# Eight plain products for the first group of batch 1, and the spatial weights' combinations made over a longer stretch

## The chip, the cores and the metric

One NeuronCore of a Trainium2 chip runs the whole program. The metric is the time of one execution on the device, in microseconds. The engines are named as the profile names them: PE is TensorE's matmuls, PEld its weight loads, DVE is VectorE, ACT is ScalarE, POOL is GpSimd, SP the engine that issues all DMAs of this kernel. Each works through its own instructions in order.

## The reference

Three layers follow one another, on 4 batches of 1088 tokens: a linear attention with polynomial features (4 heads of 32), a gated mixture layer (128 to 1024 to 128, shifted tokens), and a gMLP, the part that the change is in:

```python
h = np.maximum(x @ w_in, 0.0)                 # (4, 1088, 1024)
u, v = (h[..., :512], h[..., 512:])
mu = np.mean(v, axis=-1, keepdims=True)
var = np.mean((v - mu) ** 2, axis=-1, keepdims=True)
v_n = (v - mu) / np.sqrt(var + 1e-06)
v_s = np.einsum('ts,bsd->btd', w_spatial, v_n) + b_spatial[None, :, None]
gated = u * v_s
return (gated @ w_out).astype(np.float32)
```

The large product is `w_spatial` (1088 x 1088) with `v_n`, for each batch.

## The kernel before

**Number format.** A float32 operand is split into a high and a low part (`copy` on ScalarE makes the high part, `low` subtracts it from the whole), and `mm3` makes each product from three matmuls: low by high, high by high, high by low. `mm3` holds line 123, on which most matmul rows stand; line 126 is `copy`, line 129 is `low`.

**The spatial product.** The result is computed transposed, 128 channels `d` (four blocks) by tokens in three column chunks `c` of 384, 384 and 320 columns. The source tokens are eight blocks `k` of 128, and a tail of 64 that goes with the bias through tiles T1 and T2 (`tmm`, lines 683 and 684, and lines 537 and 538).

**Batch 0** does it plainly in twelve units `u` (`spatial`, order `ORD0`): a unit makes the window matmuls of u (left operands winH and winL, bank 3), the 24 weight matmuls of one `d` and one `c`, the tail's two, then `L539` on VectorE multiplies the accumulator by the gate, and `put_out` splits the product into high and low (`gH` on ScalarE, `gL` on VectorE). The output projection's three matmuls (left operands woL and woH; the third one needs `gL`) are kept in the list `gout` and are issued in the next unit, after its k = 6. Units 4 and 5 are (d 2, c 0) and (d 3, c 0), 6 and 7 are c 1 of the same, 8 to 11 are c 2 of all four blocks. Between the matmuls of a unit, a list `fill` places other work: the v tiles of batch 1 (`v_tile`: 512-column matmuls, ReLU, statistics on VectorE, a power on GpSimd, then `v_rest`, line 471, and a store to DRAM) two in each of the units 5 to 8, and the weight combinations of the table `W2`.

**Batches 1 to 3** work in groups (b, p), each for two channel blocks, d = p and e = p + 2. `group` is a generator, and each of its `yield`s ends a step, after which the loop at the program's end places other work. The first two column chunks and the two halves of the source tokens form a 2 by 2 block product, which a Strassen-Winograd scheme makes with seven block products for eight (`prod`; a block product is four k by three matmuls of 384 columns). The third chunk is done plainly (`plain`). A group needs

- the v blocks 11, 12, 22, 21 and their combinations 2, 1, 3, 4, made by `build(b, p, i)` in the order of `BUILD` from quadrants that `quad_load` fetches back from DRAM into slots of the buffer `VR`. Each build is a copy on ScalarE and a subtraction on GpSimd; 2 takes three sums on VectorE more, 4 takes one. The results rotate through four buffers `n1H`, `n1L`, `k0`, `k1`;
- the weights' blocks 11, 12, 21, 22 as batch 0 left them, and the combinations 1 = W12 - W11, 3 = W22 - W12, 2 = W11 + 3 and 4 = W21 - 2 for each of the four k (`ctile`). They are made once, from raw float32 weights that are loaded a second time: for each k, `first_load` and `first_sums` make 1, `second_load` and `second_sums` make 3, 2 and 4. Combination 4 takes the place of block 12 (`wtile(k, 1)`), so it can't be made before the last plain use of column chunk 1. `tail_sums` makes the difference of the tail's first two chunks from `btail`.

Each sum is one subtraction or addition on VectorE (line 587, `tt`), followed by `parts`: a copy on ScalarE and a subtraction on GpSimd. Raw weights stand in slots of `VR`.

**Order.** The program text gives the order in which work is wanted; a planner with a timeline of its own then sets each engine's order, so that instructions near one another in the text can change places on an engine. `xsplit(2)` (four copies and four splits on VectorE, line 129) stands ahead of group (1,0). In groups with p = 0 each step also makes one v tile of the next batch.

Of the kernel before, what the change touches and what calls it, by code (L numbers as in the profile page):

```python
# [8 lines left out]
F32 = mybir.dt.float32  # L9
# [49 lines left out]
W1G = 69  # L59
W1N = 8  # L60
ORD0 = ((0, 0), (1, 0), (0, 1), (1, 1), (2, 0), (3, 0), (2, 1), (3, 1), (0, 2), (1, 2), (2, 2), (3, 2))
W2 = {4: ((1, "fl", 0), (3, "fl", 1)), 5: ((3, "fs", 0), (4, "fl", 2), (6, "fs", 1), (7, "fl", 3)),
      6: ((3, "fs", 2),), 7: ((1, "fs", 3), (2, "sl", 2)), 8: ((3, "ss", 2), (4, "sl", 0)),
      9: ((1, "ss", 0), (6, "sl", 1)), 10: ((2, "ss", 1), (7, "sl", 3)), 11: ((3, "ss", 3),)}
SSET = {2: (3, 4, 5, 6), 0: (7, 8, 5, 6), 1: (7, 8, 5, 6), 3: (7, 8, 5, 6)}
R0 = (1, 5)
R1 = 5
VW = NH * (HD + 1)
# [1 line left out]
RING = ("n1H", "n1L", "k0", "k1")  # L70
BUILD = (11, 12, 22, 21, 2, 1, 3, 4)
CHOME = {(1, 2): ("t0",), (3, 2): ("t1",), (1, 3): ("t2",), (3, 3): ("t3",), (1, 0): ("t4",), (3, 0): ("x0",),
         (1, 1): ("x1",), (3, 1): ("xrH", "xrL"), (2, 0): ("n0H",), (2, 1): ("n0L",), (2, 2): ("m14", "mx"),
         (2, 3): ("st0", "st1"), (5, NK): ("m12", "m13")}


@with_exitstack
def attn_moe_gmlp(ctx: ExitStack, tc: tile.TileContext, qT, kT, va, st, wk, wv, wr, win, wout,
# [10 lines left out]
    def sb(tag, shape, dt=F32):  # L89
        uid[0] += 1  # L90
        return pool.tile(shape, dt, tag=tag, bufs=1, name=f"{tag}_{uid[0]}")

    def bank(i):
        uid[0] += 1
        return pp.tile([128, 512], F32, tag=f"p{i}", bufs=1, name=f"p{i}_{uid[0]}")
# [3 lines left out]
    def rot(*tags):  # L99
        i = count.get(tags, 0)  # L100
        count[tags] = i + 1
        return tags[i % len(tags)]

    def m(i):
        return f"m{i}"
# [14 lines left out]
    def mm3(out_ap, lH, lL, rH, rL, first, last, late=1, skip=False):  # L120
        parts = [(lL, rH), (lH, rH), (lH, rL)]
        for n, (l, r) in enumerate(parts if late else parts[::-1]):
            TE.matmul(out_ap, lhsT=l, rhs=r, start=first and n == 0, stop=last and n == 2, skip_group_check=skip)  # L123
# [290 lines left out]
    def wtile(k, c):  # L414
        n = CH[c][1]
        for t, _ in wplace(k, c):
            if t not in wt:
                wt[t] = sb(f"w{t}", [128, S], F32R)
        return [wt[t][:, o:o + n] for t, o in wplace(k, c)]
# [161 lines left out]
    def wraw(dst, n, k):  # L581
        o = CH[n % 10 - 1][0]
        r = 128 * (k + HALF * (n // 10 - 1))
        nc.sync.dma_start(out=dst, in_=wT[r:r + 128, o:o + CMAX])

    def tt(eng, o, a, b_, op):
        return eng.tensor_tensor(out=o, in0=a, in1=b_, op=op)  # L587
# [3 lines left out]
    def stage(j):  # L591
        return VR[:, j, :CMAX]

    def first_load(k):
        raws[1, k] = [stage(j) for j in rot((3, 4), (5, 6), (7, 8))]
        for x, n in zip(raws[1, k], (11, 12)):
            wraw(x, n, k)

    def parts(n, k, src):
        H, L = ctile(n, k)  # L600
        copy(H, src)
        low(GE, L, src, H)

    def first_sums(k):
        r11, r12 = raws.pop((1, k))
        tt(VE, r11, r12, r11, ALU.subtract)
        parts(1, k, r11)

    def second_load(k):
        raws[2, k] = [stage(j) for j in SSET[k]]  # L610
        for x, n in zip(raws[2, k], (12, 22, 11, 21)):
            wraw(x, n, k)

    def second_sums(k):
        r12, r22, r11, r21 = raws.pop((2, k))
        tt(VE, r22, r22, r12, ALU.subtract)
        parts(3, k, r22)
        tt(VE, r11, r22, r11, ALU.add)
        parts(2, k, r11)
        tt(VE, r21, r21, r11, ALU.subtract)  # L620
        parts(4, k, r21)

    def tail_sums():
        H, L = ctile(5, NK)
        x, y = sb(m(10), [128, CMAX]), sb(m(11), [128, CMAX])
        nc.sync.dma_start(out=x, in_=btail[:, :CMAX])
        nc.sync.dma_start(out=y, in_=btail[:, CMAX:2 * CMAX])
        tt(VE, x, x, y, ALU.subtract)
        parts(5, NK, x)
        VE.tensor_copy(L[64:65], H[64:65].bitcast(F32))  # L630
        copy(H[64:128], H[0:64].bitcast(F32))
# [24 lines left out]
    def group(b, p):  # L656
# [16 lines left out]
            for k in range(HALF):  # L673
                mm3(acc, v[:, 0, k], v[:, 1, k], *ctile(w, k), first and k == 0, k == HALF - 1, 0, True)

        def plain(acc, a, first):
            v = vset[b, p, a]
            for k in range(HALF):
                mm3(acc, v[:, 0, k], v[:, 1, k], *wtile(k + HALF * (a % 10 - 1), NCH - 1), first and k == 0, False, 0, True)

        def tmm(acc, d, W):
            T1, T2 = tl[b, d]
# [19 lines left out]
                gout.pop(0)()  # L702

        d, e = p, p + 2
        X = bank(0)[:, :CMAX]
        prod(X, 11, 11, True)
        m1 = snap(X)
# [260 lines left out]
    for u, (d, c) in enumerate(ORD0):  # L968
        if u < EARLY:
            continue  # L970
        fill = {}

        def add(k, fn, *a):
            fill.setdefault(k, []).append(lambda: fn(*a))

        for k in range(WB[u] if u < len(WB) else 0):
            add(k, wstep)
        if u == EARLY:
            add(0, xsplit, 1)
        for n, j in enumerate({5: (0, 1), 6: (2, 3), 7: (4, 5), 8: (6, 7)}.get(u, ())):  # L980
            add(2 + 3 * n, v_rest)
            add(2 + 3 * n, v_tile, 1, j)
        for k, fn, *a in W2.get(u, ()):
            add(k, {"fl": first_load, "fs": first_sums, "sl": second_load, "ss": second_sums}[fn], *a)
        if u == 9:
            add(2, v_rest)
            for n in (11, 12):
                add(2, quad_load, 1, 0, n)
        if u == 10:
            add(2, tails, 1, 0, vtail[:, 0])  # L990
            add(4, build, 1, 0, 0)
        if u == 11:
            add(1, build, 1, 0, 1)
            for n in (22, 21):
                add(7, quad_load, 1, 0, n)
        spatial(0, d, c, fill)
    assert wi[0] >= len(worder) and not pending_raw
    groups = [(b, p) for b in range(1, B) for p in range(2)]
    for gi, (b, p) in enumerate(groups):
        nxt = groups[gi + 1] if gi + 1 < len(groups) else None  # L1000
        if gi == 0:
            build(1, 0, 2)
            tails(1, 2, vtail[:, 0])
            build(1, 0, 3)
            tail_sums()
        if p == 0 and b + 1 < B:
            xsplit(b + 1)
        for st, _ in enumerate(group(b, p)):
            if st < 4:
                build(b, p, st + 4)  # L1010
            elif nxt:
                build(*nxt, st - 4)
            if nxt:
                if st in (1, 2):
                    quad_load(*nxt, (11, 12)[st - 1])
                if st in (3, 4):
                    quad_load(*nxt, (22, 21)[st - 3])
                if st in (3, 4):
                    tails(nxt[0], nxt[1] + 2 * (st - 3), vtail[:, 0])
            v_rest()  # L1020
            if b + 1 < B:
                if p == 0:
                    v_tile(b + 1, st, (3, 7))
                elif st == 0 and b % 2:
                    v_tile(b + 1, NK, (3, 7))
    while gout:
        gout.pop(0)()
# [56 lines left out]
```

## Time and profile before

| | us |
|---|---|
| median of three runs | 466.0 |
| lowest and highest | 465.8, 466.21 |
| the profiled execution, in all | 466.96 |
| its span in the profile | 465.2 |

The profile shows one execution. Busy time is the time in which an engine has an instruction under way; a matmul's end is modelled, so matmul rows overlap and their durations are no price: the price of a matmul is read from the distance of two starts. The granted clock is the share of TensorE's full speed that it was given.

### The profile page before, as it was taken

To read this page: it belongs to the slowest core of one execution; us is meant where nothing else is said; L and a number is where in the kernel's file an instruction comes from. 1 tells how busy PE (TensorE), PEld (TensorE's weight loads), DVE (VectorE), ACT (ScalarE), POOL (GpSimd) and SP (SyncE) were. 2 spreads that over 40 slices of the span, in tenths; PEclk is the share of its full clock that TensorE was granted. 3 is DMA by queue.
4 is the path that set the end of the run, shared out by engine and by line. 5 is a ranking of instruction groups with operands and counts; after the bars stand their busy time and mean duration, and the time that the engine had idled before them with its cause. 6 is when DMAs were issued, how large, how long until landed. Compare 5 with 4: busy or idle time off the path is not lost.

```text
span 465.2 us, 7573 instructions
## 1 busy us (share of the span) xinstructions
PE 446.7 (96%) x2685; PEld 421.0 (90%) x2685; DVE 288.1 (62%) x497; ACT 264.9 (57%) x606; POOL 243.5 (52%) x287
## 2 busy tenths in 40 slices
PE   8978999999999998999999989999999999999997
PEld 7967998989998886999888889999999999999996
DVE  4599768768445796348676567884475971623523
ACT  2585769888766987675444644444464433534322
POOL 2566546586634889539554655634534633425230
PEclk9999999999999999999999989999999999999999
DMA  7973100001100111036534632312112213010001
GB/s 219 345 261 93 49 0 2 17 23 50 41 2 1 36 51 36 11 91 179 153 135 144 180 93 68 115 47 92 59 58 82 100 48 113 14 58 24 0 1 48
DMA packets 32101, 36.49 MB, mean 78 GB/s; under 512 B 2944, under 2 KB 27584, under 8 KB 32064
## 3 DMA queue, kind: packets, MB, share of 16 engines
q1 hardware_dynamic: 32064, 36.01, 24.5%
q8 instruction: 21, 0.34, 0.3%
q14 instruction: 16, 0.13, 0.1%
HBM read 27.48 MB, written 8.52 MB: 77 GB/s over the span
## 4 chain that ended last, share of the span: by engine, by line
PE 64%; DVE 11%; POOL 9%; DMA 8%; issue 3%; ACT 3%; SPq 1%; POOLq 0%; DVEq 0%; ACTq 0%
PE p L123 49%; DMA VR<-in_wT_dram 4%; PE p L397 3%; PE p L231 3%; DVE w L129 3%; PE p L269 3%; PE p L200 2%; POOL m L354 2%; DVE VR L587 1%; DVE VR L471 1%; PE p L684 1%; PE p L683 1%; PE p L252 1%; POOL w L129 1%; DMA w<-in_qT_dram 1%
## 5 line engine op out<-in xcount | busy, mean ns | idle before, releaser
L123 PE MATMUL p<-m,k 128*128 128x384 f32 (+1 forms) x288 | 65.6, 347 | 2.7 <-POOL k L144 1.6
L123 PE MATMUL p<-w,k 128*128 128x384 f32 (+1 forms) x360 | 64.6, 323 | 0.0
L354 POOL TENSOR_TENSOR m<-m 128x384 f32<-128x384 f32 (+1 forms) x48 | 42.8, 897 | 38.0 <-ACT m L351 32.4
L123 PEld LDWEIGHTS p<-w,k 128*128 128x128 f32 x360 | 59.5, 188 | 0.6
L587 DVE TENSOR_TENSOR m<-p,m 128x384 f32<-128x384 f32 (+2 forms) x37 | 18.6, 519 | 58.7 <-PE p L684 57.9
L123 PEld LDWEIGHTS p<-m,k 128*128 128x128 f32 x288 | 48.2, 189 | 6.3 <-POOL k L144 1.8
L129 POOL TENSOR_TENSOR k<-VR,k 128x512 fp32r<-128x512 f32 x26 | 35.1, 1351 | 31.7 <-ACT k L126 28.9
L129 DVE TENSOR_TENSOR w<-m,w 128x384 fp32r<-128x384 f32 (+1 forms) x44 | 32.7, 751 | 28.5 <-POOL m L354 18.4
L351 ACT ACTIVATE m<-p 128x384 f32<-128x384 f32 (+1 forms) x96 | 42.5, 471 | 11.0 <-PE p L123 8.3
L126 ACT ACTIVATE m<-m 128x384 fp32r<-128x384 f32 (+2 forms) x45 | 22.6, 503 | 39.7 <-DVE m L697 24.0
L129 DVE TENSOR_TENSOR m<-m,m 128x384 fp32r<-128x384 f32 (+1 forms) x47 | 33.5, 713 | 16.3 <-ACT m L126 11.0
L471 DVE TENSOR_SCALAR VR<-VR,mv,rs 128x512 f32<-128x512 f32 x33 | 34.1, 1039 | 12.5 <-POOL rs L468 12.2
L123 PE MATMUL p<-w,n1H 128*128 128x384 f32 (+1 forms) x192 | 41.2, 333 | 0.2 <-DVE x L539 0.2
L126 ACT ACTIVATE m<-p 128x384 f32<-128x384 f32 (+2 forms) x39 | 18.3, 471 | 32.7 <-PE p L123 23.4
L587 DVE TENSOR_TENSOR VR<-VR 128x512 f32<-128x512 f32 (+1 forms) x40 | 28.6, 714 | 13.2 <-DMA VR<-in_wT_dram 9.4
L123 PE MATMUL p<-w,n1L 128*128 128x384 f32 (+1 forms) x168 | 34.3, 325 | 0.0
L123 PEld LDWEIGHTS p<-w,n1H 128*128 128x128 f32 x192 | 33.6, 195 | 0.8 <-DVE x L539 0.5
L397 PE MATMUL p<-w,wvT 128*128 128x384 f32 (+1 forms) x88 | 34.3, 471 | 0.0
L126 ACT ACTIVATE k<-VR 128x512 fp32r<-128x512 f32 x26 | 16.3, 630 | 25.0 <-PE p L123 20.2
L123 PEld LDWEIGHTS p<-w,n1L 128*128 128x128 f32 x168 | 28.4, 188 | 0.3
L129 POOL TENSOR_TENSOR n1H<-VR,n1H 128x512 fp32r<-128x512 f32 x12 | 15.5, 1290 | 25.1 <-ACT n1H L126 25.1
L123 PE MATMUL p<-w,xs1H 128*128 128x384 f32 (+1 forms) x88 | 25.1, 339 | 2.9 <-DVE w L129 2.9
(259 smaller groups left out, 1157.3 us busy)
## 6 DMA issues: line engine op xcount, KB each, us to landing
vd<-VR SPq DMA_DIRECT2D x24, 256.0 KB, 2.0
VR<-vd SPq DMA_DIRECT2D x24, 256.0 KB, 3.0
VR<-in_wT_dram SPq DMA_DIRECT2D x24, 192.0 KB, 2.6
st<-in_wT_dram SPq DMA_DIRECT2D x16, 192.0 KB, 2.3
w<-in_kT_dram SPq DMA_DIRECT2D x8, 192.0 KB, 5.1
w<-in_qT_dram SPq DMA_DIRECT2D x8, 192.0 KB, 5.2
out_dram<-m SPq DMA_DIRECT2D x8, 192.0 KB, 1.9
st<-in_wT_dram SPq DMA_DIRECT2D x8, 160.0 KB, 2.3
```

The lines of the kernel that those rows point to most:

```text
L123: TE.matmul(out_ap, lhsT=l, rhs=r, start=first and n == 0, stop=last and n == 2, skip_group_check=skip)
L126: return SE.activation(out=dst, in_=src, func=AF.Copy)
L129: return eng.tensor_tensor(out=L, in0=src, in1=H.bitcast(F32), op=ALU.subtract)
L200: TE.matmul(wide[:, 64 * t:64 * t + 128], lhsT=src[:, cut(c, t, CH[c][0])], rhs=Sbd, start=True, stop=True)
L231: TE.matmul(kv[:, w * g:w * g + w], lhsT=kp, rhs=vt if wide else vt[:, VP * g:VP * g + VP], start=(t == 0), stop=(t == NT - 1))
L252: TE.transpose(pt[:, cut(c, t)], qp[:, t, 128 * g:128 * g + 128], idn)
L269: nd_pe[0] = TE.matmul(o.rearrange("p h c -> p (h c)"), lhsT=qt[g][:, cut(c, t)], rhs=kb[:, g], start=not wide or g == 0, stop=not wide or ...
L351: SE.activation(out=r, in_=hk, func=AF.Relu)
L354: anchor[2] = GE.tensor_tensor(out=sq, in0=r, in1=r, op=ALU.mult)
L397: TE.matmul(vvs[i], lhsT=wvT[:, f // 2], rhs=hls.pop(g), start=f == 0, stop=f == NF - 1)
L471: VE.tensor_scalar(out=v, in0=v, scalar1=mv[:, 0:1], scalar2=rs, op0=ALU.subtract, op1=ALU.mult)
L587: return eng.tensor_tensor(out=o, in0=a, in1=b_, op=op)
```

## The change

In group (1,0), `group` returns early through a new branch: for each of the two channel blocks, and for each of the two v blocks of that block, the three column chunks are done with `plain`, which now takes the chunk as an argument; with the second v block come the window, the tail, the gate and `put_out`. That makes twelve steps of twelve weight matmuls, and no combination of weights or v blocks is used in it. The builds 4 to 7 of this group are left out; the steps 2, 5, 8 and 11 each make one plain build for group (1,1), and its quadrants are loaded at other steps.

The weight combinations are made by `sums` from three raw blocks (11, 12, 22), for k = 2 in unit 6, k = 3 in unit 7, k = 0 in unit 10, and k = 1 in the second step (number 1) of group (1,0), whose raw blocks stand in m8 to m10. `tail_sums` moves from before the group to its step 3. Combination 4 is made by `last_sum` in the steps 8 to 11, from raw block 21 and the two split parts of combination 2, so with two subtractions on VectorE instead of one; `last_load`, at step 5, loads the four raw blocks 21 into m8 to m11. The homes of the combinations (`CHOME`) change places.

```diff
@@ -59,10 +59,8 @@
 W1G = 69
 W1N = 8
 ORD0 = ((0, 0), (1, 0), (0, 1), (1, 1), (2, 0), (3, 0), (2, 1), (3, 1), (0, 2), (1, 2), (2, 2), (3, 2))
-W2 = {4: ((1, "fl", 0), (3, "fl", 1)), 5: ((3, "fs", 0), (4, "fl", 2), (6, "fs", 1), (7, "fl", 3)),
-      6: ((3, "fs", 2),), 7: ((1, "fs", 3), (2, "sl", 2)), 8: ((3, "ss", 2), (4, "sl", 0)),
-      9: ((1, "ss", 0), (6, "sl", 1)), 10: ((2, "ss", 1), (7, "sl", 3)), 11: ((3, "ss", 3),)}
-SSET = {2: (3, 4, 5, 6), 0: (7, 8, 5, 6), 1: (7, 8, 5, 6), 3: (7, 8, 5, 6)}
+W2 = {4: ((2, "load", 2), (4, "load", 3)), 6: ((1, "sums", 2),), 7: ((1, "sums", 3),), 8: ((3, "load", 0),), 10: ((1, "sums", 0),), 11: ((1, "load", 1),)}
+KORD = (2, 3, 0, 1)
 R0 = (1, 5)
 R1 = 5
 VW = NH * (HD + 1)
@@ -70,8 +68,8 @@
 RING = ("n1H", "n1L", "k0", "k1")
 BUILD = (11, 12, 22, 21, 2, 1, 3, 4)
 CHOME = {(1, 2): ("t0",), (3, 2): ("t1",), (1, 3): ("t2",), (3, 3): ("t3",), (1, 0): ("t4",), (3, 0): ("x0",),
-         (1, 1): ("x1",), (3, 1): ("xrH", "xrL"), (2, 0): ("n0H",), (2, 1): ("n0L",), (2, 2): ("m14", "mx"),
-         (2, 3): ("st0", "st1"), (5, NK): ("m12", "m13")}
+         (2, 2): ("x1",), (2, 3): ("xrH", "xrL"), (2, 0): ("m14", "mx"), (1, 1): ("n0H",), (3, 1): ("n0L",),
+         (2, 1): ("st0", "st1"), (5, NK): ("m12", "m13")}
 
 
 @with_exitstack
@@ -591,9 +589,9 @@
     def stage(j):
         return VR[:, j, :CMAX]
 
-    def first_load(k):
-        raws[1, k] = [stage(j) for j in rot((3, 4), (5, 6), (7, 8))]
-        for x, n in zip(raws[1, k], (11, 12)):
+    def sums_load(k):
+        raws[k] = [sb(m(x), [128, CMAX]) for x in (8, 9, 10)] if k == 1 else [stage(x) for x in ((3, 4, 5) if k == 2 else (6, 7, 8))]
+        for x, n in zip(raws[k], (11, 12, 22)):
             wraw(x, n, k)
 
     def parts(n, k, src):
@@ -601,28 +599,29 @@
         copy(H, src)
         low(GE, L, src, H)
 
-    def first_sums(k):
-        r11, r12 = raws.pop((1, k))
-        tt(VE, r11, r12, r11, ALU.subtract)
-        parts(1, k, r11)
-
-    def second_load(k):
-        raws[2, k] = [stage(j) for j in SSET[k]]
-        for x, n in zip(raws[2, k], (12, 22, 11, 21)):
-            wraw(x, n, k)
-
-    def second_sums(k):
-        r12, r22, r11, r21 = raws.pop((2, k))
+    def sums(k):
+        r11, r12, r22 = raws.pop(k)
         tt(VE, r22, r22, r12, ALU.subtract)
         parts(3, k, r22)
+        tt(VE, r12, r12, r11, ALU.subtract)
+        parts(1, k, r12)
         tt(VE, r11, r22, r11, ALU.add)
         parts(2, k, r11)
-        tt(VE, r21, r21, r11, ALU.subtract)
-        parts(4, k, r21)
+
+    def last_load():
+        for x, k in zip((10, 11, 8, 9), KORD):
+            raws[k] = sb(m(x), [128, CMAX])
+            wraw(raws[k], 21, k)
+
+    def last_sum(k):
+        c = raws.pop(k)
+        for x in ctile(2, k):
+            tt(VE, c, c, x.bitcast(F32), ALU.subtract)
+        parts(4, k, c)
 
     def tail_sums():
         H, L = ctile(5, NK)
-        x, y = sb(m(10), [128, CMAX]), sb(m(11), [128, CMAX])
+        x, y = sb(m(8), [128, CMAX]), sb(m(9), [128, CMAX])
         nc.sync.dma_start(out=x, in_=btail[:, :CMAX])
         nc.sync.dma_start(out=y, in_=btail[:, CMAX:2 * CMAX])
         tt(VE, x, x, y, ALU.subtract)
@@ -673,10 +672,10 @@
             for k in range(HALF):
                 mm3(acc, v[:, 0, k], v[:, 1, k], *ctile(w, k), first and k == 0, k == HALF - 1, 0, True)
 
-        def plain(acc, a, first):
+        def plain(acc, a, first, c=NCH - 1):
             v = vset[b, p, a]
             for k in range(HALF):
-                mm3(acc, v[:, 0, k], v[:, 1, k], *wtile(k + HALF * (a % 10 - 1), NCH - 1), first and k == 0, False, 0, True)
+                mm3(acc, v[:, 0, k], v[:, 1, k], *wtile(k + HALF * (a % 10 - 1), c), first and k == 0, False, 0, True)
 
         def tmm(acc, d, W):
             T1, T2 = tl[b, d]
@@ -702,6 +701,22 @@
                 gout.pop(0)()
 
         d, e = p, p + 2
+        if (b, p) == (1, 0):
+            for q, pair in ((d, (11, 12)), (e, (21, 22))):
+                accs = [bank(x)[:, :CH[c][1]] for c, x in enumerate((0, 1, 6))]
+                for a in pair:
+                    for c, acc in enumerate(accs):
+                        second = a == pair[1]
+                        if second:
+                            u = pre(q, c, True)
+                        plain(acc, a, not second, c)
+                        flush()
+                        if second:
+                            tmm(acc, q, wtile(NK, c))
+                            tt(VE, u, acc, u, ALU.mult)
+                            put_out(b, q, c, u)
+                        yield
+            return
         X = bank(0)[:, :CMAX]
         prod(X, 11, 11, True)
         m1 = snap(X)
@@ -981,7 +996,7 @@
             add(2 + 3 * n, v_rest)
             add(2 + 3 * n, v_tile, 1, j)
         for k, fn, *a in W2.get(u, ()):
-            add(k, {"fl": first_load, "fs": first_sums, "sl": second_load, "ss": second_sums}[fn], *a)
+            add(k, {"load": sums_load, "sums": sums}[fn], *a)
         if u == 9:
             add(2, v_rest)
             for n in (11, 12):
@@ -999,18 +1014,28 @@
     for gi, (b, p) in enumerate(groups):
         nxt = groups[gi + 1] if gi + 1 < len(groups) else None
         if gi == 0:
+            build(1, 0, 3)
+            tails(1, 2, vtail[:, 0])
             build(1, 0, 2)
-            tails(1, 2, vtail[:, 0])
-            build(1, 0, 3)
-            tail_sums()
         if p == 0 and b + 1 < B:
             xsplit(b + 1)
         for st, _ in enumerate(group(b, p)):
-            if st < 4:
+            if gi == 0:
+                if st in (2, 5, 8, 11):
+                    build(*nxt, st // 3)
+                if st in (0, 1, 6, 7):
+                    quad_load(*nxt, {0: 11, 1: 12, 6: 22, 7: 21}[st])
+                if st in (3, 4):
+                    tails(nxt[0], nxt[1] + 2 * (st - 3), vtail[:, 0])
+                if st in (1, 3, 5):
+                    (lambda: sums(1), tail_sums, last_load)[st // 2]()
+                if st > 7:
+                    last_sum(KORD[st - 8])
+            elif st < 4:
                 build(b, p, st + 4)
             elif nxt:
                 build(*nxt, st - 4)
-            if nxt:
+            if nxt and gi:
                 if st in (1, 2):
                     quad_load(*nxt, (11, 12)[st - 1])
                 if st in (3, 4):
@@ -1019,9 +1044,9 @@
                     tails(nxt[0], nxt[1] + 2 * (st - 3), vtail[:, 0])
             v_rest()
             if b + 1 < B:
-                if p == 0:
+                if p == 0 and st < NK:
                     v_tile(b + 1, st, (3, 7))
-                elif st == 0 and b % 2:
+                elif p == 1 and st == 0 and b % 2:
                     v_tile(b + 1, NK, (3, 7))
     while gout:
         gout.pop(0)()
```

## Rows read from the trace of the kernel before

**Rows 1.** The page's first part: busy us (share of the span) and instructions.

```profile
PE 446.7 (96%) x2685; PEld 421.0 (90%) x2685; DVE 288.1 (62%) x497; ACT 264.9 (57%) x606; POOL 243.5 (52%) x287
```

**Rows 2.** Busy time by stretches, 275 to 460 us; columns as in rows 3.

```profile
275.00:460.00 185.00, 185.00 (x1104) 182.78 (x1103) 103.01 (x172) 78.22 (x159) 78.70 (x88) 1.00 0.18 57
```

**Rows 3.** Busy time by stretches around the group's start; columns in the first line.

```profile
core 0: us, PE busy (x) PEld busy (x) DVE busy (x) ACT busy (x) POOL busy (x), PEclk, DMA share, GB/s
225.00:271.64 46.64, 42.06 (x241) 38.06 (x239) 30.77 (x57) 22.78 (x51) 24.71 (x34) 1.00 0.46 143
271.64:275.28 3.64, 3.64 (x14) 3.64 (x15) 2.01 (x4) 3.04 (x8) 2.07 (x3) 0.53 0.49 144
275.28:303.20 27.92, 27.92 (x165) 27.12 (x164) 20.63 (x32) 11.69 (x22) 16.32 (x21) 1.00 0.26 83
```

**Rows 4.** Timeline of TensorE: start, us, engine, line, operation [idle before <-releaser].

```profile
227.38 0.44 PE L123 MATMUL p<-m,woL 128*128 128x384 f32 x1 [0.33 <-ACT m L126]
...
235.11 0.44 PE L123 MATMUL p<-m,woL 128*128 128x384 f32 x1 [0.74 <-ACT m L126]
...
249.56 0.44 PE L123 MATMUL p<-m,woL 128*128 128x384 f32 x1 [0.38 <-ACT m L126]
...
255.98 0.41 PE L123 MATMUL p<-m,woL 128*128 128x320 f32 x1 [0.25 <-ACT m L126]
...
261.30 0.41 PE L123 MATMUL p<-xs0H,winL 128*128 128x320 f32 x1 [0.32 <-ACT m L529]
...
263.30 0.41 PE L123 MATMUL p<-m,woH 128*128 128x320 f32 x1 [0.70 <-DVE m L129]
...
271.64 0.47 PE L123 MATMUL p<-m,woH 128*128 128x320 f32 x1 [1.86 <-DVE m L129]
```

**Rows 5.** Timeline of VectorE and GpSimd, 261 to 273 us.

```profile
261.95 0.89 DVE L587 TENSOR_TENSOR VR<-VR 128x384 f32<-128x384 f32 x1 [1.82 <-DMA VR<-in_wT_dram]
...
268.35 0.70 DVE L587 TENSOR_TENSOR m<-m,m 128x384 f32<-128x384 f32 x1 [1.01 <-DMA m<-in_btail_dram]
268.97 0.95 DVE L129 TENSOR_TENSOR xs0L<-x,xs0H 128x384 fp32r<-128x384 f32 x2
...
269.69 1.08 POOL L129 TENSOR_TENSOR m<-m,m 128x384 fp32r<-128x384 f32 x1 [1.05 <-ACT m L126]
269.84 1.34 DVE L587 TENSOR_TENSOR VR<-VR 128x384 f32<-128x384 f32 x1
271.11 0.48 DVE L129 TENSOR_TENSOR m<-m,m 128x320 fp32r<-128x320 f32 x1
...
272.15 0.89 DVE L630 CAST m<-m 1x384 fp32r<-1x384 f32 x1
```

**Rows 6.** Groups by shape, VectorE, 215-272 us: busy us, mean ns | idle before.

```profile
L587 DVE TENSOR_TENSOR VR<-VR 128x384 f32<-128x384 f32 x16 | 11.0, 687 | 9.4 <-DMA VR<-in_wT_dram 9.4
```

**Rows 7.** Timeline of TensorE and VectorE, 228 to 248 us.

```profile
228.43 0.34 PE L538 MATMUL p<-w,wrH 128*128 128x384 f32 x1
...
229.31 0.56 DVE L587 TENSOR_TENSOR VR<-VR 128x384 f32<-128x384 f32 x1
...
229.91 1.85 DVE L587 TENSOR_TENSOR VR<-VR 128x384 f32<-128x384 f32 x2
...
233.97 0.53 DVE L539 TENSOR_TENSOR m<-p,m 128x384 f32<-128x384 f32 x1
...
247.33 0.56 DVE L587 TENSOR_TENSOR VR<-VR 128x384 f32<-128x384 f32 x1 [0.86 <-DMA VR<-in_wT_dram]
```

**Rows 8.** Timeline of TensorE: twelve matmuls of 384 columns and the next start.

```profile
276.46 2.27 PE L123 MATMUL p<-w,n1L 128*128 128x384 f32 x12
278.57 0.34 PE L683 MATMUL p<-w,T 128*128 128x384 f32 x1
```

**Rows 9.** Groups by shape, VectorE, 275 to 305 us; columns as in rows 6.

```profile
L587 DVE TENSOR_TENSOR VR<-VR 128x512 f32<-128x512 f32 x5 | 3.4, 686 | 3.5 <-POOL k L129 3.5
L587 DVE TENSOR_TENSOR m<-p,m 128x384 f32<-128x384 f32 x4 | 2.1, 542 | 0.0
```

## The prediction

> **What bounds the kernel now.** I read the page first: TensorE (PE) is busy for 446.7 of 465.2 us [rows 1], so only its idle time and its clock can give anything back. The view by stretches says where that idle time lies. From 275 us to 460 us there is none: 185.00 of 185.00 us are busy [rows 2]. Between 225 and 271.64 us, which is the second half of batch 0's spatial stage and the first matmuls of batch 1, 46.64 us hold 42.06 us of work, so 4.58 us are idle [rows 3]. The rest of the 18.5 us lies ahead of 225 us, where the change does nothing.
>
> The timeline of PE then names each stop [rows 4]: seven of them, 0.33, 0.74, 0.38, 0.25, 0.32, 0.70 and 1.86 us. Six end at a matmul of the output projection (left operand woL or woH, that is, the high or low part of a gated tile); the fifth ends at a matmul with winL, which waits for ScalarE to empty a bank. So PE isn't short of weights there; it waits for the tail of the tile before: multiply by the gate (L539), copy of the high part, subtraction of the low part (both in `put_out`).
>
> The clock comes with it. After the 1.86 us stop the stretch of 271.64 to 275.28 us ran at a mean granted clock of 0.53 [rows 3], a mixture of the two levels, 2.4 and 1.2 GHz. At half speed that is 3.64 x (1 - 0.53) / 0.5 = 3.42 us, in which 1.71 us of work was lost. The stretches before and after have 1.00. The most that better cover could give back is therefore 4.58 + 1.71 = 6.29 us.
>
> Why the tiles were late is seen on VectorE [rows 5]. It works in order. The subtraction that PE awaits at 263.30 [rows 4] stood behind a weight subtraction (L587) that had itself waited 1.82 us for a DMA. Before the big stop VectorE waited 1.01 us for a row of btail (`tail_sums`), then did two splits of the next batch's x, then a weight subtraction of 1.34 us, and only then the 0.48 us that PE wanted. From 215 us on the sixteen weight subtractions took 11.0 us and waited 9.4 us for DMAs [rows 6]. The same is seen earlier [rows 7]: the accumulator of unit 5 got its last matmul at 228.43, its gate multiply ran at 233.97, with three weight subtractions in between; at 247.33 such a subtraction had waited 0.86 us for a DMA, just ahead of the 0.38 us stop.
>
> **The change part by part.**
>
> Eight products for seven. Group (1,0) had seven products of 12 matmuls of 384 columns, and for the third column chunk 48 of 320; it gets 96 of 384 and 48 of 320. Window, tail, output and v matmuls are as many as before. So 12 matmuls of 384 columns are added. Twelve such took from 276.46 to 278.57 us [rows 8]: +2.11 us, on the path, since PE has no idle time there.
>
> Off batch 0's stage. Today its units 4 to 11 hold sixteen subtractions on VectorE, sixteen copies on ScalarE, sixteen subtractions on GpSimd and 24 loads. Afterwards there are nine of each (three blocks k, in units 6, 7 and 10) and 12 loads, and `tail_sums` goes too. Each block's loads are issued one to three units ahead of their use, against one unit for all but one of today's sets, so I cost the waits for DMA on VectorE at nothing; the cover is PE's work of two units, each with 24 weight matmuls (4.2 us at the price of [rows 8]), and if it failed a wait like the 1.82 us above would return.
>
> Now each stop. The first (0.33) came from ScalarE, not from a weight subtraction: I keep it. The second (0.74) lay behind those three weight subtractions; unit 5 loses its two, but unit 6 gets three, and so does unit 7, both beside two v tiles each. I keep 0.40 in each of them: 0.80. The third goes (units 8 and 9 have no sums left), the fourth too. The fifth (0.32) waits for ScalarE, which still makes three parts in unit 10: kept. The sixth goes with its DMA wait. The seventh and the clock's fall go if VectorE does no weight work at the group's head: unit 11 has only loads left, the four x splits remain. Kept: 0.33 + 0.80 + 0.32 = 1.45 us; from 0 (all gone) to 3.0 us (the first four in full, 1.70, the fifth, and another 1 us wait for btail, which `tail_sums` still loads just ahead of its use, now at the fourth step of the group).
>
> Into group (1,0). VectorE gets three subtractions of block 1, `tail_sums` (one subtraction, one one-row copy of up to 0.89 us [rows 5]) and eight subtractions of `last_sum`. It loses four sums of v blocks at 0.686 us and four joins at 0.542 us [rows 9], 4.91 us; the gate multiplies are as many. It was busy 2.01 + 20.63 = 22.64 us between 271.64 and 303.2 us [rows 3]. With 12 subtractions at 0.56 us (a free one, 247.33 [rows 7]) it comes to 22.64 - 4.91 + 6.72 + 0.89 = 25.3 us, beside 31.56 - 1.71 + 2.11 = 31.96 us of PE: 79%. At 1.34 us each (the one beside GpSimd [rows 5]) it is 34.7 us: more than PE. The mean of all sixteen today is 0.687 us [rows 6], far nearer to the free one, so I take no stall, and keep the other end as a rival. ScalarE and GpSimd lose four v builds each and gain eight or nine smaller parts; they were busy for 14.73 and 18.39 us of the 31.56 [rows 3], and this stays below.
>
> The Trainium skill bears on that 1.34 us (SBUF — State Buffer, Who interferes with whom): VectorE with two SBUF inputs and GpSimd exclude each other for a whole instruction, the later one waiting out the earlier. The trace agrees here: GpSimd ran 269.69 to 270.77 us, the VectorE subtraction begun at 269.84 ended at 271.18. By that rule alone all twelve could collide, since each is followed by a GpSimd part of about 1 us; by the mean of the row few do.
>
> Sum. Span 465.2 - 6.29 + 2.11 + 1.45 = 462.5 us. The profiled execution was 466.96 us in all, 1.76 us around its span, and 0.96 us above the median of the runs; I take the difference, -2.73 us, off the median: 466.0 - 2.7 = 463.3 us. With no stop left it is 461.8, with 3.0 us of them 464.8.
>
> **The rivals.**
>
> The crowd moves to units 6 and 7. Six sums and four v tiles meet there, and the multiply by the gate comes late as at 233.97. For it: the 0.74 us stop had just this mixture. Against it: there VectorE and ScalarE also waited for DMAs, which the earlier loads spare. It gives the 3.0 us end, 464.8 us.
>
> The stop at the group's head stays. The four x splits still stand there, 0.55 us each, and PE's third output matmul still wants unit 11's low part. For it: two of the splits preceded the low part at 268.97 [rows 5]. Against it: without the 1.01 us wait and the 1.34 us subtraction the low part would have been 2.35 us earlier, and the stop was 1.86 us. If it stays with its clock fall: 463.3 + 1.86 + 1.71 = 466.8 us, no change that can be told.
>
> The other side: VectorE becomes the bound of group (1,0) because its added subtractions collide with GpSimd. For it: the 1.34 us row, and that every sum is followed by a GpSimd part. Against it: the mean of 0.687 us, and that `last_sum` comes in the last four steps, after the last v tile. At 34.7 us VectorE would need 2.7 us more than PE; as idle PE, with one fall of the clock at the price seen, 463.3 + 2.7 + 1.71 = 467.7 us. It decides the sign from new stops of 2.7 us on, and can be measured from 3.7 us on.
>
> **How the numbers follow.** This kernel's runs lie within 0.1% of each other, so 0.2%, or 0.93 us, is about what can be told from no change. Forecast 463.3 us (own range 461.8 to 464.8): 0.58. Crowd in units 6 and 7, 464.8: 0.16. Head stop stays, 466.8: 0.11. VectorE bound, 467.7: 0.15. The first two are faster by over 0.2%: 0.74; the third is no change; the last is slower. The range from 461.8 to 466.8 leaves out the last and a little of the first.
>
> **What would show it.** Right: 2,697 matmuls for 2,685 [rows 1]; PE idle between 225 us and the group below 2 us; granted clock 1.00 throughout 265 to 280 us; weight subtractions of batch 0's stage waiting less than 2 us for DMAs; group (1,0) without PE waits, its VectorE near 79%. Wrong: a PE wait over 1 us inside the group, a low clock in it, subtractions near 1.3 us on the mean, or a DMA wait at `tail_sums` that reaches PE.

## The result: slower by 0.7%

The changed kernel takes 469.71 us (median of four runs, 469.12 to 470.0); the kernel before took 466.11 us beside it (465.8 to 467.35). The ratio is 1.0071, with a 95% interval of 1.005 to 1.0091. The forecast was 463.3 us, faster, with a range up to 466.8 us. The profiled execution took 470.0 us, its span 468.2 us, 3.0 us more than before. The page's first lines:

```profile
span 468.2 us, 7568 instructions
...
PE 448.5 (96%) x2697; PEld 424.5 (91%) x2697; DVE 286.6 (61%) x493; ACT 262.2 (56%) x602; POOL 240.4 (51%) x283
```

The 12 matmuls more are there. Busy time by stretches of the changed kernel, cut where units 4 and 11 end and where the large stop of TensorE ends:

```profile
core 0: us, PE busy (x) PEld busy (x) DVE busy (x) ACT busy (x) POOL busy (x), PEclk, DMA share, GB/s
...
221.24:265.38 44.14, 41.07 (x243) 39.13 (x244) 27.27 (x47) 20.40 (x46) 21.46 (x30) 1.00 0.41 134
265.38:272.65 7.27, 4.24 (x24) 3.72 (x23) 6.77 (x8) 2.71 (x6) 5.43 (x5) 0.96 0.08 23
272.65:282.00 9.35, 9.35 (x39) 9.22 (x40) 7.16 (x13) 2.93 (x6) 4.23 (x7) 0.67 0.35 113
...
300.00:460.00 160.00, 160.00 (x963) 158.85 (x962) 80.65 (x133) 65.92 (x136) 64.15 (x68) 1.00 0.16 52
```

TensorE's idle time hasn't gone. Between 221 and 272.65 us it is 3.07 + 3.03 = 6.10 us, where [rows 3] had 4.58. From 265.38 to 272.65 us VectorE is busy for 6.77 of 7.27 us while TensorE stands still for 3.03 us: VectorE works, but not at what TensorE wants. The clock fell again and for longer: 9.35 x (1 - 0.67) / 0.5 = 6.17 us at the lower level, 3.09 us of work lost, against 1.71. The stops, from TensorE's timeline (four of them over 0.5 us, where [rows 4] had seven of all sizes):

```profile
222.12 0.44 PE L121 MATMUL p<-xrL,woH 128*128 128x384 f32 x1 [0.88 <-DVE xrL L127]
...
229.46 0.44 PE L121 MATMUL p<-m,woL 128*128 128x384 f32 x1 [1.64 <-ACT m L124]
...
237.00 0.44 PE L121 MATMUL p<-m,woL 128*128 128x384 f32 x1 [0.55 <-ACT m L124]
...
272.65 0.63 PE L121 MATMUL p<-m,woH 128*128 128x320 f32 x1 [3.03 <-DVE m L127]
```

What the last one waited for is in the timeline of all engines at the head of group (1,0). L585 is `tt`, here the sums; L127 is `low`; L582 is a load of raw weights; `m<-m,xrH` is the first subtraction of `last_sum(3)`:

```profile
259.89 2.06 SPq L582 DMA_DIRECT2D m<-in_wT_dram  x4
...
261.41 0.49 DVE L537 TENSOR_TENSOR m<-p,m 128x320 f32<-128x320 f32 x1 [3.28 <-ACT n1L L124]
...
263.78 0.46 ACT L124 ACTIVATE m<-m 128x320 fp32r<-128x320 f32 x1
...
265.88 0.56 DVE L585 TENSOR_TENSOR m<-m,m 128x384 f32<-128x384 f32 x1 [2.62 <-DMA m<-in_wT_dram]
266.35 0.95 DVE L127 TENSOR_TENSOR xs0L<-x,xs0H 128x384 fp32r<-128x384 f32 x2
...
267.14 1.06 POOL L127 TENSOR_TENSOR n0L<-m,n0L 128x384 fp32r<-128x384 f32 x1 [3.56 <-ACT n0L L124]
267.23 1.38 DVE L585 TENSOR_TENSOR m<-m,xrH 128x384 f32<-128x384 f32 x1
...
268.15 3.15 POOL L127 TENSOR_TENSOR k<-VR,k 128x512 fp32r<-128x512 f32 x2
...
268.53 1.64 DVE L585 TENSOR_TENSOR m<-m,m 128x384 f32<-128x384 f32 x1
...
270.10 1.28 DVE L127 TENSOR_TENSOR xs0L<-x,xs0H 128x64 fp32r<-128x64 f32 x1
...
271.30 1.29 DVE L127 TENSOR_TENSOR m<-m,m 128x320 fp32r<-128x320 f32 x1
```

The high part of unit 10's tile was ready at 264.24 (263.78 + 0.46); the split at 271.30 needed nothing else, and came 7 us later. Ahead of it VectorE's queue had a subtraction of block 1 that waited 2.62 us for its load, another of block 1, the first one of `last_sum(3)`, and the x splits. Beside GpSimd's parts and its two v builds the last two of these sums, the last x split and the split itself took 1.28 to 1.64 us each; a free sum takes 0.56 us. In the program text block 1's sums belong to the group's second step and `last_sum(3)` to its tenth: the planner had taken both forward, ahead of unit 10's split and of unit 11's gate multiply, which ran at 273.72.

It did the same in batch 0. The text has the sums of k = 2 and 3 in units 6 and 7; VectorE ran these six before unit 4's gate multiply (L537 at 228.23), and four of them collided with GpSimd's parts. The three of k = 0, which the text has in unit 10, ran before unit 5's gate multiply (L537 at 235.86):

```profile
219.08 1.84 DVE L585 TENSOR_TENSOR VR<-VR 128x384 f32<-128x384 f32 x2
220.84 1.22 DVE L127 TENSOR_TENSOR xrL<-x,xrH 128x384 fp32r<-128x384 f32 x1
221.99 3.94 DVE L585 TENSOR_TENSOR VR<-VR 128x384 f32<-128x384 f32 x3
...
228.23 0.56 DVE L537 TENSOR_TENSOR m<-p,m 128x384 f32<-128x384 f32 x1
...
230.91 0.54 DVE L585 TENSOR_TENSOR VR<-VR 128x384 f32<-128x384 f32 x1
...
233.97 1.36 DVE L585 TENSOR_TENSOR VR<-VR 128x384 f32<-128x384 f32 x1
...
235.86 0.53 DVE L537 TENSOR_TENSOR m<-p,m 128x384 f32<-128x384 f32 x1
```

### The profile page after: what moved, and what is told of

Same layout as the page of the kernel before. It is cut to its first block, busy times and chain, and to the rows that moved or that the text cites. A ratio compares the mean times of both kernels' runs of the same rounds, so it can differ in the third digit from the quotient of the medians.

```text
span 468.2 us, 7568 instructions
## 1 busy us (share of the span) xinstructions
PE 448.5 (96%) x2697; PEld 424.5 (91%) x2697; DVE 286.6 (61%) x493; ACT 262.2 (56%) x602; POOL 240.4 (51%) x283
## 4 chain that ended last, share of the span: by engine, by line
PE 67%; DVE 13%; DMA 6%; POOL 6%; ACT 3%; issue 3%; SPq 1%; DVEq 0%; ACTq 0%; POOLq 0%
PE p L121 54%; PE p L395 3%; DVE w L127 3%; PE p L267 2%; POOL m L352 2%; PE p L229 2%; PE p L198 2%; DMA w<-in_wk_dram 1%; PE p L683 1%; PE p L682 1%; DMA w<-in_qT_dram 1%; PE p L250 1%; DVE VR L585 1%; DVE VR L469 1%; DVE w L137 1%
## 5 line engine op out<-in xcount | busy, mean ns | idle before, releaser
L121 PE MATMUL p<-w,k 128*128 128x384 f32 (+1 forms) x384 | 69.3, 324 | 0.0
L121 PEld LDWEIGHTS p<-w,k 128*128 128x128 f32 x384 | 63.5, 188 | 0.7
L585 DVE TENSOR_TENSOR m<-p,m 128x384 f32<-128x384 f32 (+2 forms) x37 | 18.7, 519 | 61.5 <-PE p L683 60.7
L127 POOL TENSOR_TENSOR k<-VR,k 128x512 fp32r<-128x512 f32 x24 | 32.6, 1363 | 35.1 <-ACT k L124 32.3
L127 DVE TENSOR_TENSOR w<-m,w 128x384 fp32r<-128x384 f32 (+1 forms) x44 | 32.7, 750 | 28.5 <-POOL m L352 18.4
L127 DVE TENSOR_TENSOR m<-m,m 128x384 fp32r<-128x384 f32 (+1 forms) x47 | 33.6, 715 | 19.0 <-ACT m L124 13.9
L121 PE MATMUL p<-w,n1H 128*128 128x384 f32 (+1 forms) x204 | 44.6, 340 | 0.2 <-DVE x L537 0.2
L469 DVE TENSOR_SCALAR VR<-VR,mv,rs 128x512 f32<-128x512 f32 x33 | 28.2, 861 | 16.2 <-POOL rs L466 15.9
L121 PEld LDWEIGHTS p<-w,n1H 128*128 128x128 f32 x204 | 36.8, 200 | 0.8 <-DVE x L537 0.5
L121 PE MATMUL p<-w,n1L 128*128 128x384 f32 (+1 forms) x180 | 36.8, 326 | 0.0
L121 PEld LDWEIGHTS p<-w,n1L 128*128 128x128 f32 x180 | 30.6, 188 | 0.2
L465 POOL TENSOR_SCALAR rs<-mv 128x1 f32<-128x1 f32 x34 | 9.9, 292 | 37.4 <-DVE mv L464 34.7
L121 PE MATMUL p<-m,woH 128*128 128x384 f32 (+1 forms) x86 | 25.4, 337 | 3.1 <-DVE m L127 3.0
L127 POOL TENSOR_TENSOR n1H<-VR,n1H 128x512 fp32r<-128x512 f32 x11 | 14.4, 1311 | 26.1 <-ACT n1H L124 26.1
```

The source lines that it names most:

```text
L127: return eng.tensor_tensor(out=L, in0=src, in1=H.bitcast(F32), op=ALU.subtract)
L465: GE.tensor_scalar(out=rs, in0=mv[:, 1:2], scalar1=1e-6, scalar2=None, op0=ALU.add)
L469: VE.tensor_scalar(out=v, in0=v, scalar1=mv[:, 0:1], scalar2=rs, op0=ALU.subtract, op1=ALU.mult)
```

## The experiments

Each kernel was timed beside the kernel before; the third column has that one's median. It differs by up to 0.9 us from round to round, so a difference of two kernels from different rounds is that uncertain.

| kernel | median us | before, beside it | ratio, 95% interval |
|---|---|---|---|
| the change | 469.71 | 466.11 | 1.0071 (1.005 to 1.0091) |
| block 1's sums held | 468.44 | 466.57 | 1.0048 (1.003 to 1.0066) |
| all sums held | 461.05 | 466.57 | 0.988 (0.9862 to 0.9898) |
| plain group alone | 467.41 | 466.57 | 1.0012 (1.0002 to 1.0023) |
| the change, 12 matmuls less | 467.83 | 466.57 | 1.0031 (1.0018 to 1.0044) |
| the group's sums held | 464.15 | 467.05 | 0.9939 (0.992 to 0.9957) |
| batch 0's sums held | 463.83 | 467.05 | 0.9928 (0.9912 to 0.9944) |
| before, sums held | 463.94 | 467.05 | 0.9927 (0.991 to 0.9945) |
| last sums held | 466.57 | 467.05 | 0.9987 (0.9976 to 0.9999) |
| no loads at the head | 467.54 | 466.84 | 1.0015 (0.9999 to 1.0032) |
| all held, 12 matmuls less | 458.9 | 466.84 | 0.9833 (0.9808 to 0.9858) |

The theory after the result: the planner takes any weight sum forward to where its operands seem to be there, ahead of the gate multiply or the split of a tile, and TensorE waits behind it. The rivals: it is the collisions of VectorE with GpSimd wherever the sums stand, the loads, or the added matmuls.

The tool for most of them is the kernel's own helper `behind(anchors, fn, ...)`: the instructions that `fn` issues may not be placed before those named. It changes no work, only the earliest place. The anchor is the low-part split that `put_out` issued last.

**Block 1's sums held.**

```diff
-        low(VE, gL, g, gH)
+        last_low[0] = low(VE, gL, g, gH)
...
+    low11 = list(last_low)
...
-                    (lambda: sums(1), tail_sums, last_load)[st // 2]()
+                    (lambda: behind(low11, sums, 1), tail_sums, last_load)[st // 2]()
```

> The changed kernel, with the three sums of weight block 1 allowed to start only behind the low-part split of batch 0's last tile (unit 11). Queue theory (the planner put the sums of block 1, with their 2.62 us wait for a DMA, ahead of the split that TensorE needs on VectorE): the 3.03 us stop of TensorE at 272.65 us falls below 0.5 us and the clock stays at 1.00, so 469.7 - 3.0 - 3.1 = 463.6 us, between 463 and 465.5. Rival, collisions of VectorE with GpSimd's v builds at that place (the x splits and the hoisted last sums remain there): the stop stays above 1.5 us with its clock fall, at least 467 us.

It took 468.44 us: the time is in the rival's band, but the stop fell to 1.12 us, between the two. TensorE's and VectorE's timelines show the wait moved:

```profile
266.88 0.93 DVE L586 TENSOR_TENSOR m<-m,xrH 128x384 f32<-128x384 f32 x1 [2.23 <-DMA m<-in_wT_dram]
...
269.49 0.42 PE L121 MATMUL p<-m,woH 128*128 128x320 f32 x1 [1.12 <-DVE m L127]
...
277.85 2.13 DVE L586 TENSOR_TENSOR m<-m,x 128x384 f32<-128x384 f32 x2 [2.90 <-DMA m<-in_wT_dram]
...
284.19 0.56 DVE L586 TENSOR_TENSOR m<-m,st 128x384 f32<-128x384 f32 x1 [2.02 <-DMA m<-in_wT_dram]
...
286.33 0.44 PE L121 MATMUL p<-m,woL 128*128 128x384 f32 x1 [2.45 <-ACT m L124]
```

The stop at the head fell from 3.03 to 1.12 us and the clock held at 1.00. But the last sums were still free: one of them, `m<-m,xrH`, now waited 2.23 us for its load at the head, others 2.90 and 2.02 us inside the group, and TensorE had a new stop of 2.45 us. The theory was right about the place and too narrow: block 1 is one of several sets.

**All sums held.** Besides the edit above:

```diff
+    def held(k):
+        behind(list(last_low), sums, k)
...
-            add(k, {"load": sums_load, "sums": sums}[fn], *a)
+            add(k, {"load": sums_load, "sums": held}[fn], *a)
...
-                    last_sum(KORD[st - 8])
+                    behind(list(last_low), last_sum, KORD[st - 8])
```

> The changed kernel, with every set of sums (k = 2, 3, 0 in batch 0's units, block 1, and the four last sums) held behind the low-part split of the tile issued just before it. Queue theory: besides the stop at the group's head, the three earlier stops (0.88, 1.64 and 0.55 us at 222, 229 and 237 us) shrink too, as the sums of k = 2 and 3 no longer run in units 4 and 5: 1.5 to 3 us below the kernel with block 1 alone held, 461 to 463.5 us. Rival (the sums crowd units 6 and 7 wherever they go): no better than that kernel, within 1 us of it.

461.05 us: 8.7 us faster than the change as it stands (9.1 us by their distances from the kernel before), and 1.2% faster than the kernel before. Its timelines:

```profile
229.30 0.56 DVE L127 TENSOR_TENSOR m<-m,m 128x384 fp32r<-128x384 f32 x1
229.78 1.74 DVE L586 TENSOR_TENSOR VR<-VR 128x384 f32<-128x384 f32 x3
...
278.46 0.44 PE L121 MATMUL p<-m,woL 128*128 128x384 f32 x1 [0.45 <-ACT m L124]
```

From 220 us on, the 0.45 us at 278.46 is the only stop of TensorE left, and the clock is 1.00 throughout. The three sums of k = 2 run right behind a tile's split. They are faster there as well, as the groups by shape show, first of the changed kernel (215 to 240 us), then of this one (215 to 265 us):

```profile
L585 DVE TENSOR_TENSOR VR<-VR 128x384 f32<-128x384 f32 x9 | 8.7, 967 | 1.3 <-DMA VR<-in_wT_dram 1.2
```

```profile
L586 DVE TENSOR_TENSOR VR<-VR 128x384 f32<-128x384 f32 x9 | 5.3, 585 | 0.2
```

Nine sums take 8.7 us in the one and 5.3 us in the other. So the collisions were real, but they came with the place: in units 4 and 5 the sums of three blocks stood together, beside the GpSimd parts of one another and beside the splits of batch 0's last weights. The Trainium skill (SBUF — State Buffer, Who interferes with whom) says that a VectorE instruction with two SBUF inputs contends with a GpSimd one that reads SBUF, and that the ports they share are an exclusive lock. The trace agrees: at the head GpSimd's part ran from 267.14 to 268.20, and the sum begun at 267.23 ended at 268.61, 0.41 us after it, as the sum of [rows 5] did (270.77 and 271.18); on the mean it was 0.967 against 0.585 us a sum.

**The plain group alone.** The kernel before, with the new branch of `group` and the builds and quadrants that go with it; `W2`, `SSET`, `CHOME` and the sums are the old ones.

> The kernel before with only the first part of the change: group (1,0) in eight plain products, the combinations made at their old places. Left out: block 12 has been replaced by combination 4 by then, so the second column chunk of this group is computed with wrong weights of the same shape. Queue theory: the 12 matmuls cost 2.1 us and the stop at the head stays as it was: 466.1 + 2.1 = 468.2 us, 467.5 to 469. Rival (the plain steps themselves bring stops, or the twelve are hidden): over 470, or under 467 us.

467.41 us, 0.8 us over the kernel before (466.57 beside it), 0.1 us under the expected band. The plain group isn't where the time was lost. It cost less than its matmuls; in the profiled execution the stop at the head, expected to stay, shrank from 1.86 to 0.70 us and the clock held (why it shrank wasn't tried):

```profile
270.37 0.41 PE L123 MATMUL p<-m,woH 128*128 128x320 f32 x1 [0.70 <-DVE m L129]
```

**The change without 12 matmuls, and all held without them.**

```diff
-            for k in range(HALF):
+            for k in range(HALF - (c == 0)):
```

> The changed kernel without the fourth source block of the first column chunk in group (1,0), that is, with 12 of its 144 weight matmuls left out (the result of that chunk is incomplete). If TensorE sets the end there, 469.7 - 2.1 = 467.6 us, 467 to 468.3. If VectorE sets the end of that group (the rival of the prediction that lay on the other side), no change: 469.2 us or more.

467.83 us, 1.88 us under the change. In the kernel with all sums held, the same edit:

> The kernel with all sums held, with the same 12 matmuls left out as in the run of the changed kernel without them (the first column chunk of group (1,0) is incomplete). With no stops left, TensorE alone sets the pace: 461.05 - 2.1 = 459.0 us, 458.4 to 459.5. If the plain group's matmuls hide behind something: over 460.3 us.

458.9 us, 2.15 us under it. The price of eight products for seven is thus 1.9 to 2.2 us by the medians (2.3 and 2.4 by the distances from the kernel before), wholly on the path, and it was TensorE that set the pace of the group: VectorE was busy for 17.69 of 27.00 us between 282 and 309 us in the changed kernel, and TensorE for all of them:

```profile
282.00:309.00 27.00, 27.00 (x159) 26.36 (x158) 17.69 (x36) 12.72 (x26) 13.38 (x20) 1.00 0.30 102
```

**Which sums matter.** Three kernels hold parts of the sums. The group's (block 1 and the last sums):

> The changed kernel with block 1's sums and the four last sums held behind a low-part split, batch 0's sums left free. Queue theory (any weight sum that the planner hoists ahead of a tile's gate multiply or split stops VectorE with its wait for a DMA): the stop at the group's head and the 2.45 us stop seen with block 1 alone held are gone, the early three (0.90, 1.67, 0.55 us) stay: 461.05 + 3.1 to 4 us, 464 to 465.5 us. Rival (the early stops are what matters, the head is a matter of collisions with GpSimd): 466.5 us or more.

464.15 us, as the theory had it: the early three stops (0.89, 1.66 and 0.55 us) as in the change, and from 240 us on none and no fall of the clock (columns as before):

```profile
240.00:300.00 60.00, 60.00 (x362) 58.42 (x361) 37.09 (x74) 27.10 (x58) 28.45 (x43) 1.00 0.43 141
```

Batch 0's alone:

> The changed kernel with only batch 0's sums (k = 2, 3, 0) held, the group's left free. Queue theory: the early stops go, the head stop of about 3 us and its clock fall stay: 461.05 + 3.0 + 1.7 to 3.1, 465.5 to 467.5 us. Rival (early stops matter most): 463 us or less.

463.83 us, between the two bands. The early stops went, and the one at the head was smaller than foreseen, with the clock at 1.00:

```profile
257.44 0.49 DVE L538 TENSOR_TENSOR m<-p,m 128x320 f32<-128x320 f32 x1 [1.35 <-PE p L537]
...
260.22 0.56 DVE L586 TENSOR_TENSOR m<-m,m 128x384 f32<-128x384 f32 x1 [2.29 <-DMA m<-in_wT_dram]
...
267.11 0.41 PE L121 MATMUL p<-m,woH 128*128 128x320 f32 x1 [1.46 <-DVE m L127]
...
281.32 0.45 PE L121 MATMUL p<-m,woL 128*128 128x384 f32 x1 [0.91 <-ACT m L124]
```

The last sums alone:

> The changed kernel with only the four last sums held, block 1 and batch 0 left free. Queue theory: block 1's first subtraction still waits for its load ahead of the split at the head, two hoisted last sums less: the head stop falls from 3.0 to between 1 and 2 us; 467 to 468.5 us. Rival (the last sums alone made the stops in the group): 465.5 us or less.

466.57 us, just under the band; the head stop split into 0.50 and 0.98 us. Against the change, the group's holds give 5.6 us, batch 0's 5.9, both 8.7 (6.5, 6.8 and 9.1 by the distances from the kernel before): the two halves aren't independent. One sign of it is at the head: block 1's load ended VectorE's wait 2.8 us after unit 10's gate multiply with batch 0's holds (260.22 and 257.44), and 4.5 us after it in the change (265.88 and 261.41), so the sums stood in the way for less long. Why the load came sooner there wasn't tried.

**Is it the wait for the loads or the place?** Here the seven loads at the head are gone (three in block 1's load, four in `last_load`); the sums, the first operand of `last_sum` among them, read high parts that are in SBUF anyway.

```diff
-            wraw(x, n, k)
+            if k != 1:
+                wraw(x, n, k)
...
+        if k == 1:
+            a11, a12, a22 = [x[0].bitcast(F32) for x in (wtile(k, 0), wtile(k, 1), wtile(k + HALF, 1))]
...
-            wraw(raws[k], 21, k)
...
+        s = wtile(k + HALF, 0)[0].bitcast(F32)
```

> The changed kernel without the seven loads of raw weights in and just before group (1,0): block 1's sums and the last sums read the high parts that stand in SBUF from batch 0 (the low parts are left out of these combinations). The planner still places them ahead of the split that TensorE needs. If the wait for the loads is what made the stop (2.62 us of VectorE), the 3.03 us stop falls below 1 us: 469.7 - 2 to 3 - 3.1 = 463.5 to 465.5 us. If the sums' mere place ahead of the split does, with their collisions with GpSimd, the stop stays above 1.5 us: 467 us or more.

467.54 us. The stop at the head fell from 3.03 to 1.78 us, with one of 0.39 us after it, and the clock held in the profiled execution:

```profile
265.39 1.36 DVE L585 TENSOR_TENSOR m<-w,x 128x384 f32<-128x384 f32 x1 [2.83 <-POOL n0L L127]
266.67 2.39 DVE L127 TENSOR_TENSOR xs0L<-x,xs0H 128x384 fp32r<-128x384 f32 x2
268.98 1.64 DVE L585 TENSOR_TENSOR m<-m,x 128x384 f32<-128x384 f32 x1
...
271.88 0.41 PE L121 MATMUL p<-m,woH 128*128 128x320 f32 x1 [1.78 <-DVE m L127]
```

With no load to wait for, a last sum waits 2.83 us for GpSimd instead: it writes over the buffer (m10) that GpSimd's part of block 1 (`n0L`) still reads, and unit 10's split still comes late, at 271.35. So sums that stand ahead of the split hold it up without any load, in a queue that works in order. What the wait for the loads alone is worth this run doesn't tell, since a wait of the same length took its place; the stops are 0.9 us shorter by it.

**The kernel before, with its sixteen sums held** (`behind(list(last_low), fn, k)` around `first_sums` and `second_sums`):

> The kernel before, seven products, with its sixteen sums held in the same way. Queue theory: the order on VectorE was the kernel's fault before as well, so its stops shrink too, from 4.6 us and a clock fall to 1 to 3 us: 461.5 to 464 us; it can't reach the held changed kernel's place at the head, where two sets of sums and the tail's wait for btail still stand. Rival (it needs both parts of the change): 465.5 us or more.

463.94 us, 0.7% under the kernel before. Its stops between 215 and 261 us are gone. Those at the head are 1.84 and 0.80 us, and the clock fell there in the profiled execution (0.76 on the mean of 261 to 275 us); one of 0.37 us follows in the group:

```profile
261.00:275.00 14.00, 11.37 (x51) 10.24 (x50) 9.61 (x14) 6.89 (x17) 7.88 (x9) 0.76 0.43 125
...
266.15 0.41 PE L123 MATMUL p<-m,woH 128*128 128x320 f32 x1 [1.84 <-DVE m L129]
...
270.03 0.63 PE L123 MATMUL p<-m,woH 128*128 128x320 f32 x1 [0.80 <-DVE m L129]
```

So the old kernel had the same fault. At its head, besides the rows of [rows 5], a sum of k = 3 had waited 2.67 us for its load ahead of unit 10's split:

```profile
266.31 0.56 DVE L587 TENSOR_TENSOR VR<-VR 128x384 f32<-128x384 f32 x1 [2.67 <-DMA VR<-in_wT_dram]
```

Holding alone is worth 3.1 us there, and the change on top of it another 2.9 us (2.4 by the distances from the kernel before). The kernel with all sums held, eight products and the new buffers, is the fastest that ran with all its work in it.

## Why the prediction was wrong

- **The step that failed** is this one: "The seventh and the clock's fall go if VectorE does no weight work at the group's head: unit 11 has only loads left". The prediction took the place of a sum in the program text for its place in time. The planner put block 1's first two sums and a last sum at the head, and the stop grew from 1.86 to 3.03 us instead of going; the clock's loss grew from 1.71 to 3.09 us. Holding the sums at their places, and nothing else, took 8.7 us off: the step's condition, once made true, gives what the prediction wanted of it and more.
- **Units 6 and 7** were to hold 0.80 us of stops, and the first stop to stay at 0.33 us. It is the same mistake: the sums ran in units 4 and 5, with stops of 0.88, 1.64 and 0.55 us. Held, units 6 and 7 bear six sums and four v tiles without a stop, so the rival of the crowd falls too.
- **The waits for loads**, costed at nothing, were 2.62 us at the head and 1.23 us in batch 0's stage. The cover counted on, one to three units, was gone because the sums had moved towards their loads. What this wait alone did to TensorE stays open: without the loads the sums still stopped it for 1.78 and 0.39 us.
- **The most that better cover could give back**, 6.29 us, was too low. The span with all sums held is 6.4 us shorter than before although it has 2.1 us of matmuls more: some 8.5 us came back. The idle column that the sum was read from doesn't hold all of TensorE's waits (below).
- **Eight for seven** at 2.11 us was right (1.88 and 2.15 us by the medians).
- **The rival on the other side** (VectorE bound in the group, 467.7 us) had the sign and came nearest in time, but not the mechanism: TensorE set the pace there, and what collided did so at the head and in units 4 and 5. The rival of the stop that stays had the place; it took the old size for it.
- **The noise** was taken from three runs within 0.1% of each other. Seventeen executions of the kernel before, beside four of the experiments, took 466.22 to 468.93 us.
- **The sum afterwards.** Span +3.0 us. By the columns it would be matmuls +2.1, stops +1.5 (6.10 against 4.60 from 200 us on) and clock +1.4: 5.0, or 2.0 too many. The starts of the matmuls resolve it. Let every distance from one start to the next between 200 and 300 us count by what it exceeds the distance in a stretch without waits (0.147, 0.175 and 0.230 us for 320, 384 and 512 columns, the medians of the changed kernel from 300 to 456 us). Then TensorE lost 10.3 us there before and 11.3 us after, stops and clock together: 2.1 + 1.0 makes 3.1. With all sums held it lost 2.2 us.

## What to carry to other kernels

Where a planner orders the queues, a line's place in the program is a wish and not a time: before costing a moved step at nothing, ask what keeps it from being taken forward, and if it is only its operands, name the instruction that it must stand behind. Work without a near deadline (here the sums, which no product of group (1,0) reads) should be tied behind the short chain that the bounding engine waits for; on an engine that works in order this was worth more here (8.7 us) than the algorithmic choice that it accompanied cost (2 us). A stop that goes away at one place is looked for at the next wait of the same queue: holding one set of sums moved 2.45 us of it into the group.

## What the runs showed of the hardware that was not expected

- A VectorE sum or split with both inputs in SBUF that starts inside one of GpSimd's splits (L127) ends at a fixed distance behind it: in the changed kernel's trace all 25 of 384 columns end 0.41 to 0.42 us after GpSimd's, and take up to 1.65 us for 0.56 free. Those with one input in PSUM (`p`) aren't held up: GpSimd's build ran from 403.43 to 404.96, a join begun in it took 0.54 us, and the split behind the join 1.18:

```profile
403.43 1.53 POOL L127 TENSOR_TENSOR k<-VR,k 128x512 fp32r<-128x512 f32 x1 [0.64 <-POOL wrH L127]
403.74 0.54 DVE L585 TENSOR_TENSOR m<-p,m 128x384 f32<-128x384 f32 x1
404.21 1.18 DVE L127 TENSOR_TENSOR m<-m,m 128x384 fp32r<-128x384 f32 x1
```

- The idle column understates a stop. At a granted clock of 1.00 a matmul of 384 columns starts 0.176 us after the last one [rows 8], but its modelled length is 0.34 us, so a stop is counted some 0.17 us short, and one under that isn't seen. In the kernel before, two matmuls of the output projection take from 235.39 to 235.99 us, 0.60 where 0.35 would do, with no idle time shown:

```profile
235.39 0.76 PE L123 MATMUL p<-m,woH 128*128 128x384 f32 x2
235.99 0.69 PE L123 MATMUL p<-w,m 128*128 128x384 f32 x3
```

  From before to the kernel with all sums held the idle time of the whole span fell by 4.4 us (18.5 to 14.1) and the clock's loss by 1.7, the matmuls cost 2.1, and yet the span fell by 6.4 us (465.2 to 458.8): 2.4 us more than the two columns hold.
- The clock's fall isn't the same in every execution of one kernel. The four of the changed kernel had mean granted clocks of 0.991, 0.995, 0.996 and 1.000 and took 470.0, 469.56, 469.12 and 469.85 us: the one with no fall was no faster. The 3.09 us lost to it in the profiled execution are thus not a fixed part of the 3.6 us, and what took their place in the fourth is open.
